# Moving casts, DMA transposes, weight loads and weight scalings to other places in the issue order of a fused attention and feed-forward kernel

## The chip, the cores and the metric

The kernel runs on one core of a Trainium2 chip. The metric is the device time of one execution in microseconds (us), lower is better. The program is one stream of instructions per engine, and each engine works through its own stream in order. The engines are TensorE (PE in the profile, with PEld for its weight loads), VectorE (DVE), ScalarE (ACT), GpSimd (POOL) and SyncE (SP). DMAs are issued by POOL (a software queue, q0) and by SP (a hardware queue, q1) and share 16 DMA engines.

## The reference

```python
# attention, 8 batches x 12 heads x 448 positions x 64, all float32
scores = (q @ k.T) / sqrt(64)
m = max(scores);  e = exp(scores - m)
attn = e / (sum(e) + exp(-m) + 1e-9)          # "softmax off by one"
x = (attn @ v) rearranged to (8*448, 768)
# feed-forward block on x
xn = x / sqrt(mean(x*x) + 1e-6) * rms_g
g = xn @ w_gate;  val = xn @ w_val            # 768 -> 1536
out = (g * sigmoid(g) * val) @ w_out          # 1536 -> 768
```

## The kernel before

The kernel interleaves two jobs on TensorE. The spine is the feed-forward part: for each batch b and each of 12 column blocks m, a gate group and a value group of six matmuls (`emit_A`); after every second batch the output groups (`emit_B`). Between these groups stand the attention steps of later batches: scores, attention products, transposes. The weights w_gate and w_val are multiplied by the gain of the norm in place, on the chip (`scale_w`).

```python
def scale_w(n, eng):                      # one 128x768 piece of w_gate or w_val, times gain, in place
    for _ in range(n):
        half, part, dk = w_cast.pop(0)
        w = (wg_bf, wv_bf)[part][:, dk, half * WB:(half + 1) * WB]
        ...
            eng.tensor_scalar(out=w, in0=w, scalar1=gain[:, dk:dk + 1], scalar2=None, op0=ALU.mult)

def cast_qkv(n, i, eng): ...              # q, k or v of head group n: float32 -> bf16, on POOL
def turn_qk(n): ...                       # two DMA transposes issued by SP: q and k of group n -> qk_t
def load_w_o(i): ...                      # one third of w_out, float32 -> bf16 on the way, issued by POOL
def emit_root(b): ...                     # 1/sqrt of the row sums of batch b: one pow on POOL
def emit_scale(b, c): ...                 # x of batch b times that root, on VectorE
```

When a thing is issued is decided by a list of (time, function) pairs. The times are a model's, not the chip's: the loop adds 1.13 for each gate or value group and issues what is due.

```python
now = 0.0
for t, f in ffn:                          # t = 1.13 for emit_A, 1.92 for emit_B
    ...
    while ops and ops[0][0] <= now:
        ops.pop(0)[1]()
    f()
    ...
    now += t
```

So a number in that list fixes only the order in each engine's stream. POOL, for example, runs whatever is next as soon as its inputs are there. What matters here of the list before (head groups 6, 7 and 8 are the three groups of the third batch; `NG` is 3; `emit_T` is a transpose of one pair of heads on TensorE; pairs 12 and 13 use it, pair 14 is the first to read a `qk_t` of `turn_qk`):

```python
for j, t0 in enumerate((0.0, 2.3, 4.9, 7.5, 11.6, 14.2, 19.6, 22.5)):
    ops.append((t0, lambda j=j: emit_T(NP + j)))
...
ops.append((19.2, lambda: (emit_stats(1, 1), emit_root(1))))       # the second root
...
for i in range(KD):                                                # KD = 6
    ops.append((9.6 + 0.5 * i, lambda: scale_w(1, V)))             # second half of w_gate
ops.append((14.65, lambda: scale_w(KD, V)))                        # second half of w_val, six at once
...
             (14.3, lambda: (cast_qkv(NG + 2, 2, G), loads(2 * NG + 1))),              # loads 7
             (19.3, lambda: (cast_qkv(2 * NG, 2, G), loads(2 * NG + 2))),              # loads 8
             (23.0, lambda: casts(2 * NG + 1)), (25.0, lambda: turn_qk(2 * NG + 1)),   # group 7
             (27.5, lambda: casts(2 * NG + 2)), (29.5, lambda: turn_qk(2 * NG + 2))):  # group 8
...
for i in range(KF // 4):
    ops.append((20.0 + 0.01 * i, lambda i=i: load_w_o(i)))
```

## Time and profile before

| | before |
|---|---|
| median of the first 3 runs | 488.11 us (487.27 to 488.70) |
| span in the profile | 484.9 us |
| PE busy | 461.1 us |
| two long stops of PE, 50 to 140 us | 2.6 and 7.1 us |

The busy times of the page of the kernel before, and its row of the granted TensorE clock in 40 slices (tenths of full speed):

```profile
PE 461.1 (95%) x4043; PEld 248.0 (51%) x4048; DVE 238.8 (49%) x621; ACT 249.9 (52%) x365; POOL 94.4 (19%) x109
...
PEclk9999989979999999999999999999999999999999
```

PE is busy for 95% of the span, so only PE's idle time and PE's slow time can be won. The clock row has an 8 and a 7, in slices 6 and 9 (12.1 us each): 61 to 73 and 97 to 109 us. Who PE waited for, between 50 and 140 us of the kernel before, in total us, number of waits and longest wait:

```profile
PE s_ps L205 <- DMA qk_t<-k_bf: 7.1, 1, 7.1
PE v_ps L309 <- DVE wv_bf L121: 2.6, 1, 2.6
PE s_ps L205 <- DVE pair_t_102 L181: 0.8, 1, 0.8
PE v_ps L309 <- DVE ht_sb L320: 0.3, 1, 0.3
```

In time the stop for `wv_bf` comes first, and the text calls it the first stop. Now each stop from close by. The timeline of PE in the kernel before, around the first stop (start, us, engine, line, operation, what it writes and reads, and in brackets the idle time before it and what ended it):

```profile
62.72 1.30 PE L309 MATMUL g_ps<-xnt_sb,wg_bf 128*128 128x448 bf16 x6
...
68.20 2.38 PE L309 MATMUL v_ps<-xnt_sb,wv_bf 128*128 128x448 bf16 x6 [2.57 <-DVE wv_bf L121]
70.51 0.93 PE L205 MATMUL s_ps<-pair_t_106 64*128 64x448 bf16 x4
71.37 1.58 PE L309 MATMUL g_ps<-xnt_sb,wg_bf 128*128 128x448 bf16 x6
```

A group of six takes 1.3 us at full clock. After the stop the value group takes 2.38 us: the clock had fallen. VectorE's timeline shows why the weights came late. The six scalings are issued in one block, and this block stands behind a copy (L181) and two sums of squares (L261):

```profile
65.17 0.62 DVE L181 COPY pair_t_106<-qkt_ps 128x896 bf16<-128x896 bf16 x1
...
66.37 0.69 DVE L261 CUSTOM_DVE_ANT_0 xsq<-x_sb 112x512 bf16<-112x512 bf16 x1
...
67.11 0.69 DVE L261 CUSTOM_DVE_ANT_0 xsq<-x_sb 112x512 bf16<-112x512 bf16 x1
...
67.72 2.06 DVE L121 TENSOR_SCALAR wv_bf<-wv_bf,gain 128x768 bf16<-128x768 bf16 x6
```

The second stop is a DMA transpose. This is the chain of waits of the kernel before from 88 to 109 us, in order of time (start, us, what):

```profile
88.10 0.98 POOL k_bf L154
...
89.54 15.67 DMA qk_t<-k_bf
...
105.25 0.93 PE s_ps L205 x4
106.18 2.35 PE v_ps L309 x6
```

The transpose was under way for 15.67 us; over the whole execution the DMA view has a median of 3.5 us for the same kind. The DMA view of 86 to 97 us says what it shared the engines with (queue: packets, MB, share of the 16 engines' time; then the issues with their us to landing):

```profile
q0 software_dynamic: 1141, 2.18, 100.2%
q1 hardware_dynamic: 514, 0.13, 8.9%
...
wo_bf<-in_moe_w_out_dram POOLq DMA_DIRECT2D x2, 768.0 KB, 16.5
...
qk_t<-k_bf SPq DMA_TRANSPOSE x1, 15.7
```

The packets of the software queue, that is w_out and the last of group 8's loads, add up to all of the engines' time. The transposes' packets are small (0.13 MB in 514 packets is about 250 bytes each, against 1.9 KB in the software queue). The Trainium skill ("DMA: Bandwidth & Descriptors", Queues, rings and completion order) says that each DMA engine takes turns between its queues packet by packet. It would follow that small packets beside large ones get a small part of the time.

### The profile page before, as it was taken

To read this page: it belongs to the slowest core of one execution; us is meant where nothing else is said; L and a number is where in the kernel's file an instruction comes from. 1 tells how busy PE (TensorE), PEld (TensorE's weight loads), DVE (VectorE), ACT (ScalarE), POOL (GpSimd) and SP (SyncE) were. 2 spreads that over 40 slices of the span, in tenths; PEclk is the share of its full clock that TensorE was granted. 3 is DMA by queue.
4 is the path that set the end of the run, shared out by engine and by line. 5 is a ranking of instruction groups with operands and counts; after the bars stand their busy time and mean duration, and the time that the engine had idled before them with its cause. 6 is when DMAs were issued, how large, how long until landed. Compare 5 with 4: busy or idle time off the path is not lost.

```text
span 484.9 us, 9818 instructions
## 1 busy us (share of the span) xinstructions
PE 461.1 (95%) x4043; PEld 248.0 (51%) x4048; DVE 238.8 (49%) x621; ACT 249.9 (52%) x365; POOL 94.4 (19%) x109
## 2 busy tenths in 40 slices
PE   7989979949999999999999999999999999999996
PEld 3554535514555554555455554545455555555563
DVE  5576578414644146755644136765753147655200
ACT  3977845615555665454556554555556562222221
POOL 7434403603303022313003012304000000000000
PEclk9999989979999999999999999999999999999999
DMA  7999940999619989288009879179104320200133
GB/s 131 226 228 162 197 97 22 218 221 204 142 32 232 164 218 222 45 194 190 1 18 233 182 178 225 24 164 209 27 2 109 93 86 3 57 1 0 34 97 97
DMA packets 86776, 60.47 MB, mean 125 GB/s; under 512 B 50646, under 2 KB 81692, under 8 KB 86732
## 3 DMA queue, kind: packets, MB, share of 16 engines
q1 hardware_dynamic: 73820, 43.60, 41.4%
q0 software_dynamic: 12912, 16.26, 18.0%
q8 instruction: 31, 0.51, 0.4%
q14 instruction: 13, 0.11, 0.1%
HBM read 47.19 MB, written 11.01 MB: 120 GB/s over the span
## 4 chain that ended last, share of the span: by engine, by line
PE 80%; DVE 6%; DMA 4%; POOL 4%; issue 4%; ACT 2%; POOLq 0%; DVEq 0%
PE o_ps L334 23%; PE v_ps L309 20%; PE g_ps L309 15%; PE u_ps L235 8%; PE s_ps L205 7%; PE s_ps L309 5%; DMA qk_t<-k_bf 3%; DVE xsq L261 2%; DMA v_f<-in_v_dram 1%; DVE x_sb L239 1%; ACT t_sb L313 1%; POOL v_sb_117 L154 1%; DVE ht_sb L320 1%; POOL v_f L143 1%; PE qkt_ps L178 1%
## 5 line engine op out<-in xcount | busy, mean ns | idle before, releaser
L309 PE MATMUL v_ps<-xnt_sb,wv_bf 128*128 128x448 bf16 x576 | 127.0, 357 | 4.4 <-DVE wv_bf L121 2.6
L334 PE MATMUL o_ps<-wo_bf,ht_sb 128*128 128x384 bf16 x672 | 116.5, 326 | 0.0
L309 PE MATMUL g_ps<-xnt_sb,wg_bf 128*128 128x448 bf16 x444 | 96.8, 354 | 0.7 <-DVE silu_4291 L315 0.6
L334 PEld LDWEIGHTS <-ht_sb 128*128 128x128 bf16 x672 | 62.6, 98 | 46.2 <-issue 7.8
L309 PEld LDWEIGHTS <-wv_bf 128*128 128x128 bf16 x576 | 53.0, 98 | 57.9 <-issue 11.4
L309 PEld LDWEIGHTS <-wg_bf 128*128 128x128 bf16 x576 | 52.3, 98 | 54.8 <-issue 12.2
L313 ACT ACTIVATE t_sb<-g_ps 128x448 f32<-128x448 f32 x74 | 40.2, 544 | 70.5 <-PE g_ps L309 70.2
L210 ACT ACTIVATE p_sb_114<-s_ps 112x896 bf16<-112x896 f32 x64 | 55.9, 915 | 22.9 <-PE s_ps L205 22.9
L210 ACT ACTIVATE p_sb_108<-s_ps 112x896 bf16<-112x896 f32 x64 | 55.8, 915 | 16.9 <-PE s_ps L205 16.7
L337 ACT ACTIVATE out_sb<-o_ps 128x384 f32<-128x384 f32 x56 | 27.4, 490 | 65.7 <-PE o_ps L334 58.3
L210 ACT ACTIVATE p_sb_111<-s_ps 112x896 bf16<-112x896 f32 x64 | 55.9, 916 | 9.8 <-PE s_ps L205 9.6
L238 DVE RECIPROCAL recip<-u_ps 112x4 f32<-112x4 f32 x96 | 17.0, 177 | 83.9 <-PE u_ps L235 83.9
L205 PE MATMUL s_ps<-qk_t 64*128 64x448 bf16 x272 | 37.9, 357 | 7.1 <-DMA qk_t<-k_bf 7.1
L239 DVE TENSOR_TENSOR x_sb<-u_ps,recip 112x256 bf16<-112x256 f32 x96 | 40.8, 425 | 3.3
L292 POOL TENSOR_TENSOR rinv<-ms,neghalf 112x4 f32<-112x4 f32 x8 | 8.3, 1032 | 164.6 <-DVE ms L286 148.5
L154 POOL CAST q_bf<-q_f 112x1024 bf16<-112x1024 f32 x17 | 17.7, 1042 | 109.7 <-DMA q_f<-in_q_dram 97.3
L261 DVE CUSTOM_DVE_ANT_0 xsq<-x_sb 112x256 bf16<-112x256 bf16 (+3 forms) x62 | 34.7, 560 | 1.6
L313 ACT ACTIVATE t_sb<-s_ps 128x448 f32<-128x448 f32 x22 | 11.9, 543 | 38.5 <-PE s_ps L309 33.3
L309 PE MATMUL s_ps<-xnt_sb,wg_bf 128*128 128x448 bf16 x132 | 28.6, 352 | 0.0
L235 PEld LDWEIGHTS <-p_sb_111 112*128 112x128 bf16 (+1 forms) x512 | 20.4, 99 | 6.0 <-issue 1.6
L235 PEld LDWEIGHTS <-p_sb_114 112*128 112x128 bf16 (+1 forms) x512 | 19.9, 97 | 6.0 <-ACT p_sb_114 L210 0.9
L235 PEld LDWEIGHTS <-p_sb_108 112*128 112x128 bf16 (+1 forms) x512 | 19.4, 98 | 6.9 <-issue 3.0
(278 smaller groups left out, 381.2 us busy)
## 6 DMA issues: line engine op xcount, KB each, us to landing
q_f<-in_q_dram SPq DMA_DIRECT2D x15, 448.0 KB, 4.7
k_f<-in_k_dram SPq DMA_DIRECT2D x15, 448.0 KB, 5.8
v_f<-in_v_dram SPq DMA_DIRECT2D x15, 448.0 KB, 7.2
v_f<-in_v_dram POOLq DMA_DIRECT2D x9, 448.0 KB, 7.6
out_dram<-out_sb SPq DMA_DIRECT2D x8, 336.0 KB, 2.8
wg_bf<-in_moe_w_gate_dram POOLq DMA_DIRECT2D x2, 1152.0 KB, 14.6
wv_bf<-in_moe_w_val_dram POOLq DMA_DIRECT2D x2, 1152.0 KB, 13.7
wo_bf<-in_moe_w_out_dram POOLq DMA_DIRECT2D x3, 768.0 KB, 14.8
```

The source lines that it names most:

```text
L154: eng.tensor_copy(out=dst, in_=staged[n, i].rearrange("p h c d -> p c h d"))
L205: nc.tensor.matmul(s_ps[:, hh, 0:S], lhsT=k_t[r, k0:k0 + 128], rhs=qs[r], start=True, stop=True)
L210: nc.scalar.activation(out=p_v, in_=s_ps[0:P, :, 0:S], func=AF.Exp, scale=scale)
L235: nc.tensor.matmul(u_ps[:, qc, :], lhsT=p_sb[0:K, q0:q0 + 128], rhs=v_sb[0:K, c, h, :], start=(c == 0), stop=(c == C - 1))
L238: nc.vector.reciprocal(out=recip, in_=u_ps[0:P, :, D:E1])
L239: nc.vector.tensor_tensor(out=x_tiles[b][:, :, h * D:(h + 1) * D], in0=u_ps[0:P, :, 0:D], in1=recip.to_broadcast([P, C, D]), op=ALU.mult)
L261: nc.vector.tensor_tensor_reduce(out=xsq[:, 0:n], in0=x_c, in1=x_c, scale=1.0, scalar=0.0, op0=ALU.mult, op1=ALU.add, accum_out=acc)
L292: nc.gpsimd.tensor_tensor(out=rinv, in0=ms, in1=neghalf, op=ALU.pow)
L309: nc.tensor.matmul(ps[:, 0:S], lhsT=w[:, dk, m * 128:(m + 1) * 128], rhs=xnt_tiles[b][:, :, dk, :], start=(dk == 0), stop=(dk == KD - 1))
L313: nc.scalar.activation(out=t, in_=ps[:, 0:S], func=AF.Tanh, scale=0.5)
L334: nc.tensor.matmul(o_ps[:, 0:HN], lhsT=ht_tiles[b2][:, fk, c * 128:(c + 1) * 128], rhs=wo_bf[:, fk, n * HN:(n + 1) * HN], start=(fk == 0), ...
L337: nc.scalar.activation(out=o_sb[:, n * HN:(n + 1) * HN], in_=o_ps[:, 0:HN], func=AF.Copy, scale=0.5)
```

## The change

Its intent: let the casts and DMA transposes of the third batch's later groups go ahead of the second root and of the w_out load, and spread the scalings of the second weight halves over several groups. No arithmetic is added or removed. The whole diff, without its context lines:

```diff
-    for j, t0 in enumerate((0.0, 2.3, 4.9, 7.5, 11.6, 14.2, 19.6, 22.5)):
+    for j, t0 in enumerate((0.0, 2.3, 4.9, 7.5, 11.6, 14.2, 18.4, 22.5)):
...
-        ops.append((9.6 + 0.5 * i, lambda: scale_w(1, V)))
-    ops.append((14.65, lambda: scale_w(KD, V)))
+        ops.append((8.6 + 0.5 * i, lambda: scale_w(1, V)))
+        ops.append((11.8 + 0.45 * i, lambda: scale_w(1, V)))
...
-                 (19.3, lambda: (cast_qkv(2 * NG, 2, G), loads(2 * NG + 2))),
-                 (23.0, lambda: casts(2 * NG + 1)), (25.0, lambda: turn_qk(2 * NG + 1)),
-                 (27.5, lambda: casts(2 * NG + 2)), (29.5, lambda: turn_qk(2 * NG + 2))):
+                 (16.0, lambda: (cast_qkv(2 * NG, 2, G), casts(2 * NG + 1))),
+                 (16.1, lambda: loads(2 * NG + 2)), (18.0, lambda: turn_qk(2 * NG + 1)),
+                 (20.0, lambda: casts(2 * NG + 2)), (22.0, lambda: turn_qk(2 * NG + 2))):
...
-        ops.append((20.0 + 0.01 * i, lambda i=i: load_w_o(i)))
+        ops.append((22.1 + 0.01 * i, lambda i=i: load_w_o(i)))
```

## The prediction

> **What bounds it now.** TensorE: the busy table gives PE 461.1 of 484.9 us, the chain of waits is 80% PE. The view of PE's waits shows two long ones between 50 and 140 us:
>
> 1. At 65.6 us PE stops 2.57 us for the scaled second half of w_val. In the VectorE timeline the x6 scalings (2.06 us) stand behind a PSUM copy and two sums of squares (0.69 us each). Then PE runs cold: the next three groups take 2.31, 0.86 and 1.42 us start to start instead of 1.23, 0.48 and 1.15: 1.7 us. Cost 4.3 us.
> 2. At 98.1 us PE stops 7.1 us for qk_t, the DMA transpose of k of head group 7. Issued at 89.54 us, it landed 15.67 us later (median 3.5), beside three w_out loads (768 KB each) and group 8's loads. The cold restart adds 0.39+0.98+0.40+0.12 = 1.9 us. Cost 9.0 us.
>
> The Trainium skill ("TensorE: Matmul & The Clock Gate", Part 1) says that an idle PE falls to half clock and needs some 3.4 us of work to recover; the windows agree: 0.50 to 0.60 granted for about 4 us after each stop, else 1.00.
>
> **What the change does.** Only issue order moves.
>
> - Group 7's casts (POOL, 1.04 us each) no longer stand behind the second root, for which POOL idled 23.6 us. DMA falls quiet at 65 us, so casts run at about 62 to 66, transposes start at 63 to 66 and land by 72, over 20 us before use. Group 8's follow the root (about 77), go before the w_out loads, and are needed near 110. Stop 2 should vanish: -9.0 us.
> - The w_val scalings come before the copy and the squares; two stay behind the last silu. Alone, that would leave 0.4 us of stop 1. But four POOL casts now lie inside 60 to 66 us. The skill ("SBUF — State Buffer", two separate sides) calls the POOL/VectorE port pair an exclusive lock; this trace agrees in part: three row scalings beside a cast (81.9 us) took 1.60 us instead of 1.0. I leave 1.0 us, too short to chill PE: -3.3 us.
> - Pair 12's transpose comes one group earlier. That removes a 0.76 us stop (81.55), but its PSUM buffer is wanted again by the second attention product after it, behind silu and copy: a new stop of about 1.0 us near 74. With group 8's casts beside the x scalings, net +0.6 us.
>
> Later stages should only shift.
>
> **Prediction.** 488.1 - 9.0 - 3.3 + 0.6 = 476.4 us, 8 in 10 between 473.5 and 480.5. Chances: faster by over 2% 0.85, within 2% 0.14, slower 0.01.
>
> **What would show each step.** (1) PE's waits: none on qk_t. (2) qk_t's first transposes issued near 63 to 66 us, landing in under 8 us. (3) A wait for w_val under 1.2 us, no cold groups after it. (4) A wait of 0.5 to 1.5 us near 74 on pair 12's PSUM buffer. (5) PE busy falls by about 3.6 us (cold matmuls); the rest of the gain is idle time. (6) From 138 us on, the old timeline shifted by about 12 us.
>
> **What would make it wrong.** Casts in VectorE's tightest stretch delaying silu and copies by over 1 us each; PE chilled there again (near 479); group 8's transposes caught by the w_out loads past 109 us (above 481); group 9's loads, now beside w_out, landing late.

## The result and the profile after

| | before | after |
|---|---|---|
| median of 4 runs | 487.69 us | 472.94 us |
| lowest and highest | 486.45, 488.70 | 472.61, 475.53 |
| ratio of the means | | 0.971 (0.967 to 0.975) |
| span in the profile | 484.9 us | 470.8 us |
| PE busy | 461.1 us | 456.7 us |

A ratio here is the mean time of one kernel's fast runs over that of the other's of the same rounds, so it is not quite the ratio of the medians in the table. Executions over 1.5% slower than the fastest of the same kernel are left out of the means. The change is faster by 2.9%.

The page after, the same two rows:

```profile
PE 456.7 (97%) x4048; PEld 246.7 (52%) x4048; DVE 241.1 (51%) x621; ACT 249.1 (53%) x365; POOL 95.8 (20%) x109
...
PEclk9999999999999999999999999999999999999999
```

The waits of PE in the changed kernel, 50 to 140 us. Both long stops are gone, and four kinds of short ones have come:

```profile
PE v_ps L309 <- DVE ht_sb L320: 0.9, 3, 0.4
PE u_ps L235 <- DVE pair_t_102 L181: 0.6, 1, 0.6
PE xnt_ps L275 <- DVE x_sb L266: 0.4, 1, 0.4
PE s_ps L205 <- DVE pair_t_106 L181: 0.2, 1, 0.2
```

The queue of SP in the changed kernel: group 7's transposes are issued at 63.79 and 65.31 us, and they land 3.0 us later.

```profile
63.79 1.47 SPq L167 DMA_TRANSPOSE qk_t<-q_bf  x1
65.31 1.29 SPq L167 DMA_TRANSPOSE qk_t<-k_bf  x1
```

PE's timeline where the first stop was. The value group that waited starts after its predecessor without a stop of PE and takes 1.43 us, not 2.38 (the weight loads of such groups still waited 0.5 us in all for the last scalings):

```profile
60.55 1.30 PE L309 MATMUL g_ps<-xnt_sb,wg_bf 128*128 128x448 bf16 x6
...
63.29 1.43 PE L309 MATMUL v_ps<-xnt_sb,wv_bf 128*128 128x448 bf16 x6
...
72.81 0.67 PE L235 MATMUL u_ps<-v_sb_120,p_sb_114 113*128 113x65 bf16 x16 [0.57 <-DVE pair_t_102 L181]
```

The last line is the new stop for the PSUM buffer of pair 12. VectorE's timeline in the changed kernel shows the price of the earlier casts: two scalings took 1.28 us (0.74 when nothing is beside them), one sum of squares 1.31 us (0.69 before), and three scalings of x after the root 3.11 us:

```profile
63.02 1.28 DVE L121 TENSOR_SCALAR wv_bf<-wv_bf,gain 128x768 bf16<-128x768 bf16 x2
...
65.42 1.31 DVE L261 CUSTOM_DVE_ANT_0 xsq<-x_sb 112x512 bf16<-112x512 bf16 x1
...
76.90 3.11 DVE L266 TENSOR_SCALAR x_sb<-x_sb,rinv 112x768 bf16<-112x768 bf16 x3
```

How the 14.1 us between the two spans add up can be read from the starts of the same groups in the two PE timelines. The lead is the start before minus the start after:

| group | before | after | lead | gained since the row above |
|---|---|---|---|---|
| batch 0, block 2, gate | 44.08 | 41.91 | 2.17 | 2.17 |
| batch 0, block 6, gate (ahead of stop 1) | 62.72 | 60.55 | 2.17 | 0 |
| batch 0, block 8, gate (after stop 1) | 75.51 | 69.69 | 5.82 | 3.65 |
| batch 1, block 0, gate (root, pair 12) | 90.70 | 85.75 | 4.95 | -0.87 |
| batch 1, block 3, value (after stop 2) | 110.50 | 96.39 | 14.11 | 9.16 |
| end | 484.9 | 470.8 | 14.1 | 0 |

The first row is a surprise. Up to there both kernels run the same instructions, and still 2.17 us separate them. The PE timelines say when: the dummy matmul of 512 columns that follows the first scores takes 0.61 us in the kernel before and 0.39 us in the changed one, at about the same time. Before, then after:

```profile
9.61 0.61 PE L353 MATMUL warm_ps<-blank 128*128 128x512 bf16 x1
```

```profile
8.80 0.39 PE L353 MATMUL warm_ps<-blank 128*128 128x512 bf16 x1
```

The clock came up before 8 us in one and after 13 us in the other. The table of starts therefore splits the difference into 11.9 us behind the third gate group, which the change can explain, and 2.2 us before it, which must be asked about. All comparisons of traces below use "the rest": the span minus the start of that third gate group (the first row of the table).

### The profile page after: what moved, and what is told of

The parts are those of the page before. It is cut to its first block, busy times and chain, and to the rows that moved or that the text cites. A ratio compares the mean times of both kernels' runs of the same rounds, so it can differ in the third digit from the quotient of the medians.

```text
span 470.8 us, 9822 instructions
## 1 busy us (share of the span) xinstructions
PE 456.7 (97%) x4048; PEld 246.7 (52%) x4048; DVE 241.1 (51%) x621; ACT 249.1 (53%) x365; POOL 95.8 (20%) x109
## 4 chain that ended last, share of the span: by engine, by line
PE 85%; DVE 9%; ACT 4%; issue 1%; POOL 0%; DVEq 0%; ACTq 0%
PE o_ps L334 24%; PE v_ps L309 21%; PE g_ps L309 16%; PE u_ps L235 9%; PE s_ps L205 8%; PE s_ps L309 5%; DVE xsq L261 3%; DVE x_sb L239 1%; ACT p_sb_108 L210 1%; DVE ht_sb L320 1%; PE warm_ps L353 1%; ACT t_sb L313 1%; PE qkt_ps L178 1%; ACT p_sb_114 L210 1%; DVE x_sb L266 1%
## 5 line engine op out<-in xcount | busy, mean ns | idle before, releaser
L309 PE MATMUL v_ps<-xnt_sb,wv_bf 128*128 128x448 bf16 x576 | 125.0, 353 | 2.4 <-DVE ht_sb L320 2.4
```

What stands on the lines that cost most here:

```text
L309: nc.tensor.matmul(ps[:, 0:S], lhsT=w[:, dk, m * 128:(m + 1) * 128], rhs=xnt_tiles[b][:, :, dk, :], start=(dk == 0), stop=(dk == KD - 1))
```

## The experiments

Each was run beside the kernel before on the same chip. "Gain" is the mean of the kernel before's fast runs less that of its own. The rest of the kernel before is 441.1 us, the mean of two traces (440.8 and 441.4); "less rest" is the difference to that.

| run | mean | gain | rest | less rest |
|---|---|---|---|---|
| changed kernel, 15 runs in all | 473.9 | 13.3 | 428.9 and 428.5 | 12.4 |
| scalings only | 482.1 | 4.4 | 436.2 | 4.9 |
| order only | 478.5 | 8.0 | 434.2 | 6.9 |
| w_out only | 478.2 | 8.3 | 432.5 | 8.6 |
| w_out right after the root | 475.5 | 11.0 | 429.7 | 11.5 |
| pair 12 back | 473.3 | 14.4 | 429.0 | 12.2 |
| all before the root | 475.3 | 12.4 | 430.3 | 10.8 |
| scalings and w_out, 9 runs in all | 473.8 | 13.4 | 427.1 and 428.2 | 13.5 |
| the same, start filled | 473.1 | 13.9 | 428.5 | 12.6 |

For the changed kernel and for the version with two edits the gain is the mean of all their fast runs against the mean of the 46 runs of the kernel before that the experiments took, 487.2 us (for the changed kernel also its first four runs are counted). Gains of the others scatter by about 1 us, as their starts differ.

The rest is not exact either. For "pair 12 back", "all before the root" and the first run of "scalings and w_out" the trace kept is of another execution than the one read for the table (spans of 472.7, 473.9 and 472.8 us). Their rests are 428.2, 429.4 and 428.6 us, against 429.0, 430.3 and 427.1 in the table: the same kernel moves by about 1 us from trace to trace.

### Scalings only

```diff
-        ops.append((9.6 + 0.5 * i, lambda: scale_w(1, V)))
-    ops.append((14.65, lambda: scale_w(KD, V)))
+        ops.append((8.6 + 0.5 * i, lambda: scale_w(1, V)))
+        ops.append((11.8 + 0.45 * i, lambda: scale_w(1, V)))
```

> Only the spreading of the weight scalings, all else as before. Theory: the stop for w_val (2.57 us) falls to 0.5 us or less, with no cold groups after it, because no POOL casts lie in that stretch; the stop for qk_t stays at about 7 us with its cold restart. Some 4 us less than before (about 484 us). Rival (the stop is VectorE's total load, not its order): the stop is only moved to the next group and under 1 us is gained.

Measured: 481.67 us median, ratio 0.991 (0.986 to 0.996). PE's waits from 60 to 110 us; the wait for w_val is not in the list any more:

```profile
PE s_ps L205 <- DMA qk_t<-k_bf: 7.5, 1, 7.5
PE s_ps L205 <- DVE pair_t L181: 0.5, 1, 0.5
PE u_ps L235 <- DVE x_sb L239: 0.2, 1, 0.2
```

The theory holds: the first stop was a matter of order in VectorE's stream. It was not VectorE's load, which is the same here (239.1 us busy against 238.8).

### Order only

The edits of the casts, transposes and w_out loads, with the scalings and pair 12's transpose as before.

> Only the order of casts, transposes and w_out loads of the change; scalings and pair 12's transpose as before. Theory: no wait on qk_t; the stop for w_val stays and grows by up to 1 us, as casts now collide with VectorE's queue; 8 to 9 us less than before (about 479 to 480 us). Rival (the two parts need each other): less than 7 us.

Measured: 478.27 us median, ratio 0.984 (0.979 to 0.989). The second stop is gone, the first has grown. The wait of PE, and the six scalings and the second sum of squares in VectorE's timeline:

```profile
PE v_ps L309 <- DVE wv_bf L121: 4.0, 1, 4.0
```

```profile
67.14 1.40 DVE L261 CUSTOM_DVE_ANT_0 xsq<-x_sb 112x512 bf16<-112x512 bf16 x1
...
68.47 3.01 DVE L121 TENSOR_SCALAR wv_bf<-wv_bf,gain 128x768 bf16<-128x768 bf16 x6
```

The same six scalings took 2.06 us in the kernel before and 3.01 us here; the same sum of squares took 0.69 and 1.40 us. Beside the sum of squares stood two casts on POOL (66.93 to 69.44 us); beside most of the scalings (68.47 to 71.48 us) stood POOL's issuing of the three loads of group 8 (69.39 to 71.75 us). The Trainium skill ("SBUF — State Buffer", SBUF: two separate sides) says that GpSimd and VectorE share one pair of ports under an exclusive lock, for VectorE operations with two operands in SBUF or in a two-port mode. The trace agrees in what grew: it is scalings and sums of squares, while the operations with one operand in PSUM (`silu2`, `ht_sb`) kept their 0.62 us in the changed kernel too. The stop grew by 1.5 us, more than the 1 us that the theory allowed. The gain in time, 8.0 us, is at the low end of the theory's 8 to 9; in the trace the edits are worth 6.9 us. Spreading the scalings is worth 4.9 us alone and 12.4 - 6.9 = 5.5 us beside the casts. The two parts may help each other, as the longer stop says, but a difference of 0.6 us is within the scatter of the traces.

### The w_out loads only

```diff
-        ops.append((20.0 + 0.01 * i, lambda i=i: load_w_o(i)))
+        ops.append((29.6 + 0.01 * i, lambda i=i: load_w_o(i)))
```

> The kernel before with one edit: the three w_out loads go behind group 8's casts. Group 7's casts still stand behind the second root. If the w_out traffic is what made the transposes late, they land in under 8 us, by about 94 us, and the 7 us stop shrinks to 0 to 1 us: about 479 to 480 us. If instead the late casts are the cause, the stop stays above 5 us and the time within 2 us of before.

Measured: 478.4 us median, ratio 0.984 (0.978 to 0.989). Group 7's casts are still behind the root, its transposes are issued at 84.60 and 85.98 us, and PE's waits from 60 to 110 us have nothing on `qk_t`:

```profile
PE v_ps L309 <- DVE wv_bf L121: 2.6, 1, 2.6
PE s_ps L205 <- DVE pair_t L181: 0.8, 1, 0.8
```

The transposes landed after 5.6 and 5.0 us, as the theory had it, against 13.7 and 15.7 us before. The DMA view of the run, transposes issued from 84 to 87 us:

```profile
qk_t<-q_bf SPq DMA_TRANSPOSE x1, 5.6
qk_t<-k_bf SPq DMA_TRANSPOSE x1, 5.0
```

One edit of one number does what all the moved casts and transposes do for the second stop. So the late transpose was made by the w_out traffic; casts behind the root were not enough to make it.

### The w_out loads right after the root

The changed kernel with one edit:

```diff
-        ops.append((22.1 + 0.01 * i, lambda i=i: load_w_o(i)))
+        ops.append((19.5 + 0.01 * i, lambda i=i: load_w_o(i)))
```

> The changed kernel, but the w_out loads are issued right after the root, before group 8's casts. Theory: group 8's transposes now land late (over 8 us) but still before use at about 109 us, so no wait on qk_t; the x scalings, no longer beside casts, take about 1.0 to 1.6 us for the three instead of 3.1. Time the same as the changed kernel within 1 us. Rival (putting the w_out loads last is essential): a wait on qk_t of several us returns.

Measured: 475.32 us median, ratio 0.977 (0.973 to 0.981). The mean, 475.5 us, is 1.6 us above the changed kernel's: 1.0 us of it in the rest and the remainder in a late start (44.55 us), so "within 1 us" was missed in time and just met in the trace. There is no wait on `qk_t`, although group 8's transposes took 12.5 and 13.4 us to land. So either of the two moves removes the second stop by itself: the casts ahead of the root, or the w_out loads behind them. The scalings of x took less than in the changed kernel (3.11 us) but not the hoped 1.0 us. Beside them stood not a cast but POOL's issuing of the w_out loads. VectorE, then POOL:

```profile
80.02 2.14 DVE L266 TENSOR_SCALAR x_sb<-x_sb,rinv 112x768 bf16<-112x768 bf16 x3
```

```profile
79.66 2.32 POOL L125 DMA_DIRECT2D wo_bf<-in_moe_w_out_dram  x3
81.97 1.08 POOL L154 CAST q_bf<-q_f 112x1024 bf16<-112x1024 f32 x1
```

### Pair 12's transpose back

```diff
-    for j, t0 in enumerate((0.0, 2.3, 4.9, 7.5, 11.6, 14.2, 18.4, 22.5)):
+    for j, t0 in enumerate((0.0, 2.3, 4.9, 7.5, 11.6, 14.2, 19.6, 22.5)):
```

> The changed kernel with pair 12's transpose back in its old place (one group later). Theory: the 0.57 us stop for its PSUM buffer near 72.2 us goes, the old stop of about 0.8 us for the scores that read it returns; within 0.5 us of the changed kernel. If the early transpose was a mistake, this is over 0.5 us faster.

Measured: 473.44 us median, rest 429.0 us against 428.9 and 428.5. The stop of 0.57 us on the PSUM buffer went and the old one came back with 0.6 us. This part of the change is worth nothing either way.

### Everything of the third batch before the root

The changed kernel, with group 8's q and k loaded right after group 7's, its casts and transposes directly after group 7's, and the w_out loads next, all ahead of the second root in POOL's stream.

> The changed kernel, with group 8's loads, casts and transposes and the w_out loads all ahead of the second root, so that no POOL work stands beside the scalings of x. Theory (port collisions): the three x scalings take about 1.0 us instead of 3.1 and the 0.4 and 0.2 us stops after the root go, but casts of group 8 may stretch VectorE work before the root; 0.3 to 1 us faster than the changed kernel in the part after the start. Rival: POOL traffic only moves its collisions; same within 0.3 us.

Measured: 474.97 us median, ratio 0.975 (0.971 to 0.978), rest 430.3 us: 1.6 us worse than the changed kernel in this trace. The three scalings did fall to 1.08 us with nothing beside them. But POOL works in order, and the root now waited for the casts and the w_out issues ahead of it: it began at 78.46 us, 1.7 us after its input. VectorE and then PE waited for it:

```profile
79.58 1.08 DVE L266 TENSOR_SCALAR x_sb<-x_sb,rinv 112x768 bf16<-112x768 bf16 x3 [1.71 <-POOL rinv L292]
```

```profile
PE xnt_ps L275 <- DVE x_sb L266: 1.4, 1, 1.4
```

Both theories missed: the collisions at the root could be removed, but nothing was gained by this way of doing it. By how much it loses is not shown: in the second trace the rest is 0.7 us worse, and on the same chip the means are 475.3 us and, for the changed kernel, 474.6 us, with runs from 472.4 to 478.8 us.

### The two effective edits alone

The kernel before with the scalings spread and the w_out loads at 29.6, and nothing else. It was run twice, on two chips.

> The kernel before with only two of the edits: scalings spread, and w_out loads put behind group 8's casts; group 7's casts and pair 12's transpose stay where they were. If the two stops are independent, the gain is the sum of the two single ones, 4.6 and 8.3 us after the start is taken off, that is about 12.5 to 13 us: the same as the changed kernel or up to 1 us faster, since no cast lies beside the scalings. Rival (the casts ahead of the root are needed): a wait on qk_t comes back, as group 7's transposes are now needed 4 us earlier, and the time is over 477 us.

> The two-edit version (scalings spread, w_out loads last) again, beside the next kernel on one chip. Theory: between the third gate group and the first output group its trace takes about 80.9 us, 1.1 us less than the changed kernel's 81.9; its runs scatter over 2 to 3 us with the granted clock, 472 to 475 us.

Measured: medians 472.93 and 474.49 us, ratios 0.971 (0.968 to 0.973) and 0.974 (0.972 to 0.976). The two single edits add up: 4.9 + 8.6 = 13.5 us less rest, and 13.5 measured (mean of 427.1 and 428.2 us). So the two stops are independent, within the 1 us or so that the rest scatters by. From the third gate group to the first output group the two edits took 80.9 and 81.2 us, and the changed kernel 81.9 and then 81.5: the lead of 1.1 us that the theory gave them shrank to 0.3 us in the second pair of traces. In time there is no lead: 473.8 us (mean of 9) and 473.9 us (mean of 15) are level.

### The changed kernel again

It was run twice more, on two chips, without an edit.

> The changed kernel as it is, with more rounds. Theory: of the 14.1 us between the first two profiles only 11.9 us lie after the program point where the change starts; the other 2.2 us are a matter of how early the matmul clock comes up in the first 15 us, the same instructions in both kernels. So the runs of the changed kernel, like those of before, should scatter over some 2 to 3 us with the mean granted clock, and the mean gain over before should be near 12 us (about 474.5 against 486.5), not 14. Rival: the start is faster because of the change; then all its runs stay near 472.7 and the gain at 14 us.

> The changed kernel once more, on the same chip as the two-edit version, since its profile fell into a slow state last time. Theory: 1 to 1.5 us slower than the two-edit version in the mean of its fast runs; the part between the third gate group and the first output group takes 81.9 us again. If the two are level within 0.5 us here, the difference of their traces is not a gain in time.

Measured: medians 475.11 and 473.32 us, ratios 0.973 (0.970 to 0.976) and 0.972 (0.970 to 0.975), fast runs from 472.39 to 476.04 us. The gain did not stay at 14 us: with all runs it is 13.3 us. On the first chip the changed kernel was 1.3 us slower in the mean than the two edits (474.6 against 473.3 us). On the second chip the changed kernel was not slower than the two edits, as the theory had it, but 0.8 us faster in the mean (473.6 against 474.4). There all four runs of the two edits had a granted clock of 0.992 or 0.993, as a start that chilled again would leave it. The trace of one of them shows this: the clock fell back near 9 us, came up again, and fell once more at 36 us, there after stops of no more than 0.57 us. The first gate group took 2.42 us instead of 1.3:

```profile
36.87 2.42 PE L309 MATMUL g_ps<-xnt_sb,wg_bf 128*128 128x448 bf16 x6
```

One run took 775.35 us, and the profile fell on it. It serves for no comparison, but it shows how low a clock can stay. In the first line the granted clock still reads 1.00, though in that stretch groups of six matmuls took 2.45 us and more. The windows of that run (us, busy us of each engine, granted clock, DMA share, GB/s):

```profile
40.00:60.00 20.00, 19.41 (x97) 7.93 (x95) 7.93 (x19) 6.06 (x10) 3.52 (x5) 1.00 0.21 32
...
120.00:400.00 280.00, 280.00 (x1473) 122.33 (x1470) 90.10 (x226) 95.78 (x136) 34.55 (x33) 0.56 0.42 91
```

### The start filled

The two-edit version with one more line:

```diff
     warm(10)
     emit_T(0)
+    warm(3)
```

> The two-edit version with three more dummy matmuls in the 1 us gap of TensorE near 6.5 us, before the first scores. Theory (the 2 us scatter of the start is when the clock comes up, and that hangs on how full the first microseconds of TensorE are): the clock comes up before 8 us in the trace, the third gate group starts at 41.9 to 42.5 us, and the mean of the runs falls by about 1 us against the unfilled version. Rival (it hangs on chance alone): same mean and scatter within 0.5 us, or 0.3 us slower for the added work.

Measured: 472.61 us median, ratio 0.972 (0.969 to 0.974), third gate group at 41.91 us, five of six runs at a granted clock of 0.998 or more and all between 472.28 and 472.91 us; the sixth took 475.67 us. Its mean is 1.3 us below that of the unfilled version run beside it on the same chip, 0.7 us below that of all nine unfilled runs. That is the direction of the theory, but the interval overlaps, and one run escaped it. What speaks for the theory is the trace: the clock was up at 5.5 us and stayed up, where in five unfilled runs (scalings only, w_out only, w_out right after the root, the two edits again, and the kernel before again) it was up by 5.9 us and had fallen back by 9.3 us. That is one filled trace against five, so it is a likely gain, not a shown one.

### The kernel before again

> The kernel before, unchanged, for a second trace of it. Open question: 2.2 us of the difference of the first two profiles lie in the first 44 us, where both kernels run the same instructions, and in 29 runs the kernel before was under 484.5 us only once. Theory (chance of the clock): this trace starts its third gate group anywhere between 41.9 and 44.6 us; the stretch from there to the end is 440.8 us plus or minus 2, with stops of 2.6 and 7.1 us again; an early start may come with a lower granted clock (0.982) after the stops. Rival (the start of this kernel is always the slow one): 44.1 us again.

Measured: 487.27 us median, third gate group at 44.19 us (44.08 in the first trace), rest 441.4 us, stops of 2.6 and 8.0 us. The start was slow again, but not in the same way. In the first trace the clock stayed low until 13 us; here it was up at 4.8 us and fell back, as the 2.08 us stop before the first scores shows. This is PE's timeline:

```profile
4.82 0.39 PE L178 MATMUL qkt_ps<-identity,q_bf 112*64 112x112 bf16 x8
...
7.54 0.56 PE L205 MATMUL s_ps<-pair_t 64*128 64x448 bf16 x2 [2.08 <-DVE pair_t L181]
8.02 0.59 PE L178 MATMUL qkt_ps<-identity,q_bf 112*64 112x112 bf16 x8
```

So the rival was right about its 44.1 us, though two traces don't show "always", and pure chance is hard to believe: of 46 runs the kernel before was under 485 us once, while 8 of 15 runs of the changed kernel have a granted clock of 0.999 or 1.000 and lie below 473.4 us. Yet the version with two edits started late in both its traces (44.36 and 44.55 us), and that with w_out moved alone at 42.91 us; all of them run the same instructions up to there. And one kernel can start in both ways: "all before the root" has 42.4 us in the trace read above and 44.5 us in the other one. What decides between these starts stays open.

## Why the prediction was right or wrong

**The stops and their sizes: right.** The prediction took the change apart into -9.0, -3.3 and +0.6 us. The leads of the two traces give -9.16, -3.65 and +0.87 us, a sum of 11.9 us against 11.7. The cold restart was rightly counted with each stop. Without it the two stops are 9.7 us and would not have explained the gain.

**The end time: too cautious by 2.5 to 3.5 us.** 476.4 us was predicted; the first four runs have a median of 472.94 us, 0.6 us below the stated range, and all 15 fast runs a mean of 473.9 us, within it. The term that was missing from the sum is the start: 2.2 us in the first pair of traces, about 1 us in the mean of all runs (13.3 us gain less 12.4 us less rest). The other 1.6 us between 476.4 and 473.9 are the base (488.1 us was the median of three runs, the mean of 46 is 487.2) and 0.7 us more gain in the rest than the 11.7 us predicted. The prediction treated everything before 50 us as equal in both kernels. The instructions are equal, but the clock's history is not.

**What removed the second stop: right effect, one of two sufficient moves.** The prediction let the stop vanish because group 7's casts no longer stand behind the root. The run with only the w_out loads moved removes it with the casts still behind the root; the run with the w_out loads back beside group 8 removes it with the casts ahead. Each move suffices.

**The collision of casts with VectorE: right, and under-sized where it was left alone.** The prediction kept 1.0 us of the first stop for it. With spread scalings 0.6 us of stops are left (0.17 and 0.39 us), but with the block of six the stop grew to 4.0 us. At the root three scalings took 3.11 us, twice what the kernel before showed.

**The single marks.** (1) No wait on `qk_t`: right. (2) Transposes at 63.8 and 65.3 us, landing in 3.0 us: right. (3) No wait of PE for w_val (0.5 us in all of its weight loads) and no cold groups: right. (4) A stop of 0.57 us on pair 12's buffer at 72.2 us: right, at the low end. (5) PE busy fell by 4.4 us where 3.6 were expected; the rest of it fits the warmer start, which no run splits off. (6) The old timeline shifted by 14.1 us, not by 12: 2.2 us of it are the start.

## What to carry to other kernels

Where TensorE is busy throughout, look for the one or two stops that a late tile makes, and add the cold groups after each: here they were 3.6 us of 13.3. Ask first which transfer stood beside the late one; moving three weight loads that nobody needed for another 50 us did as much as reordering seven casts and four transposes. Spread a block of weight preparation over the groups ahead of its use, so that nothing unrelated stands between its last piece and the matmul that waits, and do not give POOL work that touches SBUF at the moment when VectorE is tightest.

## What the Trainium skill lacked or had wrong

- "TensorE: Matmul & The Clock Gate", Part 1, says that the clock falls after an idle window of about 3.4 us. In both traces of the kernel before and in that with only w_out moved, a stop of 2.57 us was enough: the next group took 2.33 to 2.38 us instead of 1.3. Later than 50 us, single stops of up to 1.2 us left the next group at 1.3 us. But near 36 us, in the second run of the two edits and in that with w_out right after the root, three stops of 0.35 to 0.57 us among short transposes were followed by a gate group of 2.42 us at a granted clock of 0.50; in both traces each of the kernel before and of the changed kernel the same stops were not.
- The same page names half clock, full clock and, with three busy cores, 13/16. One run of this one-core program (what other cores did is not on record) stayed at a granted clock of 0.56 from about 80 us to its end at 773 us, and the trace kept of that run, another slow execution, at 0.85 from 20 us to its end at 522 us. The nearest that the page has is a clock seen stuck at a quarter for more than 50 us; no page describes lasting states of these sizes.
- The same page calls the start's scatter run-variable and under 1% of a span. Here it was up to 2.6 us of 473 (third gate group from 41.91 to 44.55 us), which is under 1% but half as large as the gain of one of the edits. The page warns that clock events of a trace are not always to be trusted; it lacks the plain case seen here: the profile's granted clock read 1.00 from 4 to 16 us while matmuls of 512 columns took 0.61 us instead of 0.39 us. The cold start had to be read from durations.
- "SBUF — State Buffer", SBUF: two separate sides, tells of VectorE holding up the descriptor writing of POOL's DMAs. It does not spell out the opposite, which was seen too: three scalings beside the issue of the w_out loads took 2.14 us and 1.08 us with nothing beside them.
- "DMA: Bandwidth & Descriptors" says that DMA queues share the engines packet by packet, but not what this does to a transpose: one landed after 15.7 us beside the software queue's loads and after 3.0 us on quiet engines.
